# Fewer value orders on TensorE, made later, and promotions wholly on VectorE: a case of a fused attention and MLP kernel

## The chip, the cores and the metric

The kernel runs on one core of a Trainium2 chip. The time is the device time of one execution in microseconds, and all executions compared here are undisturbed ("fast"). A profile shows one execution. Its span leaves out some 1 to 2 us of the device time, so spans are compared with spans and times with times. The "granted clock" is the share of the full TensorE clock that the profile shows as let through: 1.00 is full clock, 0.50 is half clock.

## The reference, cut to what matters

```python
def _attn_ref(q, k, v, f_logit):              # 4 batches, 8 heads, 768 tokens, head size 48
    f = 1.0 / (1.0 + np.exp(-f_logit))
    for t in range(S):
        state = f[:, :, t, :, None] * state + np.einsum('bhd,bhe->bhde', k[:, :, t], v[:, :, t])
        y[:, :, t] = np.einsum('bhd,bhde->bhe', q[:, :, t], state)
# then: tokens x (heads*head size) = 3072 x 384, through an MLP of width 2048
h = x @ w_in
g = h * (1.0 / (1.0 + np.exp(-1.702 * h)))
return g @ w_out
```

The weights arrive as 64 bit numbers, which the kernel itself converts to 32 bits.

## The kernel before

The work is cut into 12 units of 256 tokens. Within a unit the recurrence is done in six levels that double the distance between query and key. In each level TensorE makes scores, VectorE multiplies them with masks ("evacuates" them), and TensorE adds scores times values into the output `y`. A "promotion" multiplies half of the queries and half of the keys by products of the gates, for the next level. Every level needs the rows of v in its own order (`vl`).

Units 0 to 3 are the "fill": the instructions of all engines run in the order of the program, the weights are still being converted (mostly on VectorE), and the MLP of finished units is woven in as "fill" matmuls where its weights are ready. In unit 0 there is no MLP to weave in yet.

The parts that the change touches:

```python
N_FILL = 3
def load_vl(n, u):                       # one order of v for unit n
    if n < N_FILL:                       # by TensorE: permutation matrix times v, copied by ScalarE
        for i, x in enumerate((0, 1) if u == 0 else (u,)):
            pt = ps.tile([P, DM], F32, tag="mm", ...)
            for g in range(NG):
                nc.tensor.matmul(pt[...], lhsT=ident[:, x::2] if u == 0 else perm[:, u - 2, :], rhs=vns[n][:, g, :], ...)
            nc.scalar.copy(vls[n, x], pt)
        return
    ...                                  # from unit 3 on: a DMA from v_tok, a copy of v in DRAM by token
def promote(l):
    if n < N_FILL:
        nc.vector.tensor_tensor(qk[:, 1], qk[:, 1], by[:, 1], ALU.mult)   # key half
        nc.gpsimd.tensor_tensor(qk[:, 0], qk[:, 0], by[:, 0], ALU.mult)   # query half
    else:
        nc.vector.tensor_tensor(qk, qk, by, ALU.mult)
    ...                                  # then ScalarE copies the keys of the next level (Kc)
def level(l):
    ...                                  # scores and sums on TensorE
    promote(l)
    t["A"] = evacuate(256, [(0, l)])     # masks on VectorE
    if n + 1 < N_FILL:
        values(l)                        # the orders of the NEXT unit
def merge(n, fill, columns, share, pieces=0, hold=0, by=1.0):
    ...                                  # deals `columns` of MLP and 5 * `pieces` conversions over the parts of unit n
```

## Time and profile before

| | before |
|---|---|
| time, median of 4 | 727.08 us (725.85 to 729.3) |
| span of the profile | 726.1 us |
| TensorE busy | 695.9 us |
| VectorE busy | 399.6 us |
| GpSimd busy | 62.2 us |
| order matmuls of v (the profile counts each fp32 matmul of the program as two) | 84 |

What bounds the kernel is worked out in the prediction below, with the lines. In a timeline line the columns are: start, length from the first to the last of the group, engine, source line, operation, output<-inputs, shapes, count, and in brackets the idle time ahead and what ended it. In the chain they are start, length and what ran. `tv` are order matmuls, `sc` scores, `y` the output sums, `t` the turning of inputs, `h` and `o` the MLP, `a`, `s`, `w_in` and `w_out` the conversions of weights.

### The profile page before, as it was taken

The page shows a single profiled execution, that of the slowest core. Times are in us where ns is not written, and L with a number is a line of the kernel's source. Part 1 is how long each engine was busy: PE and PEld are TensorE (multiplying, and loading weights), DVE is VectorE, ACT ScalarE, POOL GpSimd, SP SyncE. Part 2 cuts the span into 40 slices and gives each one's busy share as a digit, 9 for nine tenths or more (in the row PEclk, how much of TensorE's full clock was granted, in tenths as well). Part 3 has the DMA queues.
Part 4 walks back from the last instruction along what each step waited for, and adds up shares of the span by engine and source line. Part 5 has one row for each costly group of instructions (what it writes and reads, how often), then busy time and mean ns, then how long its engine had stood idle before and what let it go on. Part 6 is the DMA issues. An engine that isn't in the chain of part 4 may idle for free.

```text
span 726.1 us, 20759 instructions
## 1 busy us (share of the span) xinstructions
PE 695.9 (96%) x9236; PEld 512.4 (71%) x9236; DVE 399.6 (55%) x665; ACT 207.0 (29%) x429; POOL 62.2 (9%) x108
## 2 busy tenths in 40 slices
PE   6876998999999999999999999999999999999998
PEld 5464666677677686686686686686686686686774
DVE  3679966697685754553554554553554554352120
ACT  4443442242222222232232222232232222122120
POOL 4213121210001001001001001001001001000000
PEclk9897999999999999999999999999999999999999
DMA  8565393485126334514513624514413211100000
GB/s 213 137 154 133 78 206 99 119 196 115 47 59 165 117 100 107 136 49 105 140 47 86 152 55 103 146 44 105 133 55 86 67 34 46 34 2 18 29 0 22
DMA packets 65796, 67.88 MB, mean 93 GB/s; under 512 B 29868, under 2 KB 58284, under 8 KB 65708
## 3 DMA queue, kind: packets, MB, share of 16 engines
q1 hardware_dynamic: 65708, 66.57, 36.0%
q8 instruction: 72, 1.18, 0.7%
q14 instruction: 16, 0.13, 0.1%
HBM read 57.11 MB, written 8.26 MB: 90 GB/s over the span
## 4 chain that ended last, share of the span: by engine, by line
PE 90%; DVE 4%; DMA 2%; SPq 2%; issue 1%; ACT 1%; DVEq 0%; ACTq 0%
PE o L614 35%; PE h L598 34%; PE sc L379 7%; PE y L436 6%; PE y L560 2%; PE t L341 2%; DMA bits<-in_moe_w_out_dram 2%; PE sc L520 2%; PE tkn L502 1%; PE tv L277 1%; SPq L243 1%; DMA vn<-in_v_dram 1%; DVE s L208 0%; DVE a L215 0%; DVE w_in L217 0%
## 5 line engine op out<-in xcount | busy, mean ns | idle before, releaser
L614 PE MATMUL o<-w_out,g 128*128 128x384 f32 x768 | 265.8, 495 | 2.7 <-DVE g L604 2.7
L598 PE MATMUL h<-xT,w_in 128*128 128x256 f32 x1152 | 264.4, 383 | 0.0
L598 PEld LDWEIGHTS h<-xT,w_in 128*128 128x128 f32 x1152 | 214.2, 190 | 35.5 <-issue 3.2
L614 PEld LDWEIGHTS o<-w_out,g 128*128 128x128 f32 x768 | 142.2, 191 | 94.5 <-issue 5.6
L604 DVE TENSOR_TENSOR g<-h,sg 128x256 f32<-128x256 f32 x192 | 80.9, 423 | 147.8 <-ACT sg L603 147.1
L603 ACT ACTIVATE sg<-h 128x256 f32<-128x256 f32 x192 | 73.6, 384 | 159.3 <-PE h L598 155.6
L426 ACT COPY Kc<-X 128x512 f32<-128x512 f32 x60 | 37.7, 628 | 166.9 <-DVE X L422 126.3
L422 DVE TENSOR_TENSOR X<-X,tot 128x1024 f32<-128x1024 f32 x45 | 54.9, 1220 | 35.4 <-PE sc L379 35.3
L403 DVE TENSOR_TENSOR A<-sc,masks 128x512 f32<-128x512 f32 (+1 forms) x84 | 62.6, 755 | 8.8 <-PE sc L379 8.8
L436 PE MATMUL y<-A,vl 64*48 64x64 f32 (+1 forms) x2688 | 61.0, 232 | 0.0
L436 PEld LDWEIGHTS y<-A,vl 64*48 64x48 f32 x2688 | 51.3, 122 | 5.8 <-issue 5.7
L368 POOL TENSOR_TENSOR tot<-F 128x512 f32<-128x512 f32 x12 | 12.5, 1041 | 475.3 <-DVE st L541 469.3
L379 PEld LDWEIGHTS sc<-X,Kc 48*64 48x64 f32 x1920 | 34.4, 136 | 23.3 <-issue 21.3
L569 ACT COPY yT<-y 48x512 f32<-48x512 f32 x48 | 27.9, 580 | 73.7 <-PE y L560 73.1
L379 PE MATMUL sc<-X,Kc 48*64 48x64 f32 x1920 | 42.0, 225 | 3.2 <-ACT Kc L426 3.1
L329 DVE STREAM_TRANSPOSE X<-raw 128x1024 f32<-128x1024 f32 x18 | 36.8, 2046 | 7.5 <-PE sc L379 7.1
L379 PEld LDWEIGHTS sc<-X 48*64 48x64 f32 x768 | 19.0, 141 | 23.5 <-issue 15.8
L379 PE MATMUL sc<-X 48*64 48x128 f32 (+1 forms) x768 | 23.7, 261 | 11.4 <-DVE X L373 6.0
L373 DVE TENSOR_TENSOR X<-X,F 128x1024 f32<-128x1024 f32 x12 | 14.8, 1235 | 23.1 <-PE y L560 15.5
L422 DVE TENSOR_TENSOR X<-X,F 128x1024 f32<-128x1024 f32 x9 | 11.0, 1226 | 28.2 <-PE sc L379 28.2
L544 DVE TENSOR_TENSOR st<-st,sc 128x192 f32<-128x192 f32 x44 | 15.6, 354 | 19.6 <-PE sc L520 18.2
L368 POOL TENSOR_TENSOR tot<-tot 128x256 f32<-128x256 f32 (+4 forms) x60 | 24.2, 403 | 4.7
(49 smaller groups left out, 388.1 us busy)
## 6 DMA issues: line engine op xcount, KB each, us to landing
vl<-v_tok SPq DMA_DIRECT2D x45, 192.0 KB, 2.8
bits<-in_moe_w_out_dram SPq DMA_DIRECT2D x8, 768.0 KB, 7.2
bits<-in_moe_w_in_dram SPq DMA_DIRECT2D x8, 576.0 KB, 5.1
xT<-yT SPq DMA_DIRECT2D x24, 144.0 KB, 2.7
raw<-in_f_logit_dram SPq DMA_DIRECT2D x18, 192.0 KB
raw<-in_q_dram SPq DMA_DIRECT2D x18, 192.0 KB, 6.8
raw<-in_k_dram SPq DMA_DIRECT2D x18, 192.0 KB
v_tok<-in_v_dram SPq DMA_DIRECT2D x9, 384.0 KB, 6.9
```

Of the source, the lines that this page charges most:

```text
L329: nc.vector.transpose(out.rearrange("p (a i j) -> p a j i", a=NP, j=R), raw[:, j].rearrange("p a (j d) -> p (a j) d", j=R)[:, :, :32],)
L368: nc.gpsimd.tensor_tensor(tn, t2[:, :, 0], t2[:, :, 1], ALU.mult)
L379: nc.tensor.matmul(out[g * HS:(g + 1) * HS, h, a, :], lhsT=lhs(h, a * U + g * G), rhs=rhs(h, a * U + g * G), start=True, stop=True,)
L403: nc.vector.tensor_tensor(A[:, :, c:c + w].rearrange("p h (x t) -> p h x t", t=64), t["sc"][:, :, c:c + w].rearrange("p h (x t) -> p h x t ...
L422: nc.vector.tensor_tensor(qk, qk, by, ALU.mult)
L426: nc.scalar.copy(Kc.rearrange("p (n m) -> p n m", m=m), X[:, 2].rearrange("p (n two m) -> p n two m", two=2, m=m)[:, :, 0, :],)
L436: nc.tensor.matmul(dst(h, g, a), lhsT=vls[n, u][g * 64:(g + 1) * 64, (2 * a + h) * D:(2 * a + h + 1) * D], rhs=A(h, g, a), start=(start an ...
L569: nc.scalar.copy(yT[rows(h), :, g, :], py[columns(h, g), g])
L598: nc.tensor.matmul(ph, lhsT=w_in[:, c, ff * P:(ff + 1) * P], rhs=xTs[n][:, c, :], start=(c == 0), stop=(c == NK - 1))
L603: nc.scalar.activation(sg, ph, AF.Sigmoid, scale=1.702)
L604: nc.vector.tensor_tensor(g[ff // FG][:, ff % FG, :], ph, sg, ALU.mult)
L614: nc.tensor.matmul(t["po"], lhsT=g[ff // FG][:, ff % FG, tt * P:(tt + 1) * P], rhs=w_out[:, ff, :], start=(ff == ffs[0]), stop=(ff == ffs[ ...
```

## The change

The intent is to take work from TensorE and stop it from standing at a late v: only units 0 and 1 have their orders made by TensorE, and unit 1's are made where unit 1 begins, not inside unit 0. Unit 2's come by DMA. The query halves of the promotions go to VectorE.

```diff
+    N_TURN = 2
 def load_vl(n, u):
-        if n < N_FILL:
+        if n < N_TURN:
 ...                                     (order_v and load_vn likewise)
                 nc.vector.tensor_tensor(qk[:, 1], qk[:, 1], by[:, 1], ALU.mult)
-                nc.gpsimd.tensor_tensor(qk[:, 0], qk[:, 0], by[:, 0], ALU.mult)
+                nc.vector.tensor_tensor(qk[:, 0], qk[:, 0], by[:, 0], ALU.mult)
 ...
-            if n + 1 >= N_FILL:
-                values(l)
+            if n + 1 >= N_TURN:
+                for u in (0, 2) if l == 2 else (l,):
+                    load_vl(n + 1, u)
             promote(l)
             t["A"] = evacuate(256, [(0, l)])
-            if n + 1 < N_FILL:
-                values(l)
 ...
-        if n == 0:
-            parts.insert(2, ("-", lambda: [load_vl(0, u) for u in range(4, NV)]))
-            parts.insert(1, ("-", lambda: [load_vl(0, u) for u in (2, 3)]))
+        if n < N_TURN:
+            parts.insert(2, ("-", lambda: [load_vl(n, u) for u in range(4, NV)]))
+            parts.insert(1, ("-", lambda: [load_vl(n, u) for u in (2, 3)]))
 ...
-            parts.append((kind, lambda: (fn(), begin_q())))
+            parts.append((kind, lambda: (fn(), begin_q(), load_vl(n + 1, 0) if n + 1 < N_TURN else None)))
```

More of the change, by code (lines that the diff above doesn't have):

```diff
@@ L257, in order_v @@
     def order_v(n, engine=nc.sync):
-        if n >= NALL or n < N_FILL:
+        if n >= NALL or n < N_TURN:
             return
@@ L299, in load_vn @@
         vns[n] = (mlp if n == 1 else ld).tile([P, NG, DM], F32, tag="osb" if n == 1 else "vn", name=f"vn_{n}", bufs=1)
-        if n < N_FILL:
+        if n < N_TURN:
             b, s0 = n // NU, n % NU * U
@@ L480, in level @@
                 add(l, slot(t["A"], 0), half(LEV[l - 1], 1))
-            if n + 1 >= N_FILL:
-                values(l)
+            if n + 1 >= N_TURN:
+                for u in (0, 2) if l == 2 else (l,):
+                    load_vl(n + 1, u)
             promote(l)
             t["A"] = evacuate(256, [(0, l)])
-            if n + 1 < N_FILL:
-                values(l)
-        def values(l):
-            for u in (0, 2) if l == 2 else (l,):
-                load_vl(n + 1, u)
         for l in range(2, NL):
@@ L510, in _ @@
             add(NL, slot(t["A"], 0), half(LEV[-1], 1))
-            if n + 1 >= N_FILL:
+            if n + 1 >= N_TURN:
                 load_vl(n + 1, NL)
@@ L525, in _ @@
                             )
-            if n + 2 < N_FILL:
-                load_vn(n + 2)
-            if n + 1 >= N_FILL:
+            if n + 1 >= N_TURN:
                 load_vn(n + 1)
-            else:
-                load_vl(n + 1, NL)
             st = att.tile([P, NC, NP, D], F32, tag="st", name=f"st_{n}", bufs=2)
@@ L666, in parts_of @@
         parts = list(units[n][1])
-        if n == 0:
-            parts.insert(2, ("-", lambda: [load_vl(0, u) for u in range(4, NV)]))
-            parts.insert(1, ("-", lambda: [load_vl(0, u) for u in (2, 3)]))
+        if n < N_TURN:
+            parts.insert(2, ("-", lambda: [load_vl(n, u) for u in range(4, NV)]))
+            parts.insert(1, ("-", lambda: [load_vl(n, u) for u in (2, 3)]))
         if n + 1 < NALL:
```

## The prediction

> **What bounds the kernel now.** I read the page first, then the busy time of each engine in stretches chosen at the borders of the first units, then the chain of waits, then the timelines of VectorE, GpSimd and TensorE between 10 and 160 us. The page's slices (each 18 us) say where there is anything to win:
>
> ```profile
> PE   6876998999999999999999999999999999999998
> DVE  3679966697685754553554554553554554352120
> POOL 4213121210001001001001001001001001000000
> PEclk9897999999999999999999999999999999999999
> ```
>
> After the eighth slice TensorE is full and VectorE is about half full. TensorE is busy 695.9 of 726.1 us, so 30.2 us are idle. The stretches place them: 4.5 at the start, 5.5 in 15 to 28.5, 2.2 in 28.5 to 41, 0.4 in 41 to 53, 7.8 in 53 to 66, 1.0 in 66 to 84, 4.3 in 101 to 117, 1.2 in 135 to 160, 3.3 at the end. From 160 us the end is simply TensorE's remaining work, so whatever the change takes from the first 120 us should reach the end nearly whole.
>
> ```profile
> 15.00:28.50 13.50, 8.03 (x210) 5.04 (x206) 12.36 (x20) 5.69 (x12) 3.50 (x3) 0.87 0.86 206
> 28.50:41.00 12.50, 10.28 (x214) 6.22 (x216) 7.40 (x12) 4.37 (x9) 3.31 (x3) 0.80 0.18 55
> 53.00:66.00 13.00, 5.21 (x128) 4.72 (x127) 12.90 (x21) 4.80 (x9) 6.34 (x8) 0.63 0.66 149
> 66.00:84.00 18.00, 17.04 (x355) 11.21 (x347) 15.92 (x30) 6.47 (x16) 5.04 (x5) 0.98 0.31 89
> ```
>
> The columns after the stretch are busy us (and instructions) of TensorE's matmuls, its weight loads, VectorE, ScalarE and GpSimd, then granted clock, DMA share and GB/s. In unit 0 (4.5 to 53 us) and at the start of unit 1, VectorE sets the pace, except in 28.5 to 41, where it is only 7.4 of 12.5 us busy. The chain shows why:
>
> ```profile
> 9.81 11.14 DMA bits<-in_moe_w_out_dram
> ...
> 24.27 4.21 DMA vn<-in_v_dram
> 28.52 4.39 PE tv L277 x12
> ```
>
> Unit 0 makes the v orders of unit 1 between its levels. That v lands only at 28.5, behind a backlog of other loads, so the TensorE stands at it, and then makes twelve of them at half clock before the next scores at 32.83. VectorE is idle for 6.11 us ahead of the mask multiplication at 33.60.
>
> The second cost is in the split promotions. GpSimd rows first, then VectorE rows of the same times:
>
> ```profile
> 35.73 1.16 POOL L420 TENSOR_TENSOR X<-X,tot 128x512 f32<-128x512 f32 x1 [0.93 <-PE sc L379]
> 39.95 1.15 POOL L420 TENSOR_TENSOR X<-X,tot 128x512 f32<-128x512 f32 x1 [3.06 <-PE sc L379]
> 35.61 1.49 DVE L215 TENSOR_SCALAR a<-s 128x384 int32<-128x384 int32 x2
> 37.49 0.68 DVE L419 TENSOR_TENSOR X<-X,tot 128x512 f32<-128x512 f32 x1
> 40.10 1.21 DVE L212 TENSOR_SCALAR a<-a 128x384 int32<-128x384 int32 x1
> ```
>
> The two L215 take 0.61 together when GpSimd is quiet and one L212 takes 0.34; beside a promotion on GpSimd they take 1.49 and 1.21. The first promotion on VectorE, beside GpSimd's, takes 2.02 instead of 0.68.
>
> **What the skill says.** "SBUF — State Buffer", section "Who interferes with whom", says that VectorE and GpSimd share a port pair, held for a whole instruction while the other fully blocks; an operation with two SBUF inputs contends with a GpSimd operation that reads SBUF. The trace agrees (the rows above; mask multiplications, whose one input is in PSUM, are not stretched: 1.29 us for two at 65.09 beside GpSimd, 1.28 at 20.99). "TensorE: Matmul & The Clock Gate", section "Part 1: The HAM clock gate", says that the array falls to half clock after an idle window of about 3.4 us. The trace agrees roughly, and here a window busy for some 40% is already followed by a slow one: the granted clock is 0.50 to 0.53 in 29 to 32, in 40 to 42 and in 111 to 114. "DMA: Bandwidth & Descriptors", section "Specifications", puts efficient transfers at 512 B and above. The new staging of v moves runs of 48 floats, 192 B; in the trace such a staging landed in 6.9 us median for 384 KB, which I use.
>
> **Part 1, promotions.** VectorE gets 18 halves, each 0.68 us, with the next instruction 0.61 behind: 3.7 us a unit, 11.0 in all. It loses the stretching, which I summed row by row against the unstretched length. Unit 0: 1.34, 1.10, 0.48, 0.46, 0.88, 0.87, together 5.1. Unit 1: 1.33, 0.08, 0.96, 0.91, 0.52, 0.84, together 4.6. Unit 2: 1.30, 0.36, 0.30, 0.44, 0.43, together 2.8. So VectorE's work changes by -1.4, -0.9 and +0.9 us. The halves come ahead of the mask multiplication, so each level's masks come 0.61 later where nothing was stretched, and at level 0 about 0.65 earlier (1.36 instead of 2.02).
>
> **Part 2, v orders in unit 0.** They leave it (28 matmuls, 7 copies). I laid VectorE's order out again from 14.4 us with its own durations. Masks of level 0 end at 16.9 (17.6 now). Those of level 2 end at 24.9, as now, and those of level 3 at 28.4 instead of 34.2, because the wait for v is gone; level 5's at 36.2 instead of 42.4. TensorE then turns unit 1's inputs from about 33.7 instead of 41.9. But between those levels it now does only 1.3 us of scores and sums in each 3.9 us, below the 40%, so I expect it at half clock and charge about 2 us on the turns, which nothing hides. Unit 0's state thus comes some 6 us earlier.
>
> **Part 3, v orders in unit 1.** The first 8 matmuls (1.47 us at full clock, from the row at 11.75) fall in a 4.38 us wait of TensorE, the next 8 in one of 3.42 us; both cost nothing and keep the clock up. I take 1.4 us for that at the scores and sums after 62.94, which ran at 0.50. The last 12 cost about 2.2 us but replace 12 at nearly the same place. The four groups of 4 later in unit 1 (about 0.80 us each, 3.2 together) go. There is a side effect in the program: the fill holds for two parts, and the inserted part counts as one, so it begins one part earlier. That delays level 2's scores by about 2.4 us but takes matmuls from the levels behind. Those levels are then VectorE's (nearly 5.0 us each, now 15.9 busy of 18 in 66 to 84), so about 1 us of the gain is lost there, and is had back where the unit ends under TensorE.
>
> **Part 4, unit 2.** It loses its orders on TensorE altogether: 28 at about 0.19 are 5.3 us of work. It is the same 5.3 us as parts 2 and 3 remove net and is not added again. Its orders become DMA in unit 1: one staging and seven reads, some 2.1 MB more. In 66 to 84 the DMA share is 0.31, so there is room. They are needed only in unit 2, tens of us later. At its start, the conversion stretched to 2.31 at 106.74 loses 1.30 and the promotion adds 0.61: 0.6 earlier.
>
> **Sum.** At the end of unit 0 -6; start of unit 1 -0.65 and -1.4, total about -8; through unit 1 about -9.3 (0.8 for the group of orders ahead of its end, the rest from less fill left); unit 2 -0.6: about -10 us, so 717.5 us. TensorE's side agrees: 5.3 us less work, and some 4 to 5 us of idle time or half clock less in the first 117 us.
>
> **Rivals.** (a) VectorE becomes the bound: promotions are serialised, and every level of units 0 and 1 is lengthened by 0.61. For it: VectorE is at 12.9 of 13 us in 53 to 66. Against it: the stretching was worth more than what is added. It would leave about -4: 723. (b) Orders by DMA get in the way: the in-order queue waits for sums of unit 1 before it can issue weights, or the 192 B runs hold the weights up. For it: queue waits on VectorE for weights are already up to 13 us, and the share is 0.81 in 84 to 101. Against it: the weights wait for the same levels in the program anyway. It would make 722 to 728. (c) The clock: fewer matmuls in unit 0 keep the array cold longer than I charged, 2 to 3 us more: 720. (d) The other way, the waits of 1.62 and 2.67 us at 103 and 109 close and the slow window at 111 goes: up to 4 more, 713.
>
> **Range and chances.** (c) and (d) are about equally likely and (a) and (b) less so, which gives 711 to 723.5. Faster by over 2% means under 712.9, which needs all of (d): 0.1. Slower by over 2% would need a new stall of 25 us, 0.01.
>
> **What would show it.** Right: no wait for v near 28 us; mask multiplication of level 3 near 28; L215, L212 and L217 at their short lengths; GpSimd with 18 fewer instructions; 56 order matmuls instead of 84; TensorE's idle time in 53 to 66 well under 7.8; all after 160 us shifted as a block by about 10. Wrong: if VectorE waits for weights or the queue waits for sums in unit 1; if TensorE's busy sum falls by less than 4; if the gain at unit 1's start is not there at 160 us.

## The result

The changed kernel took 716.7 us (median of 4, 715.02 to 716.99) against 727.08, and 716.27 us in a later control. The ratio of the fast runs is 0.9849, 95% interval 0.982 to 0.9878. Such a ratio is the mean time of one kernel's fast runs over that of the other's of the same rounds, so it is not quite the ratio of the quoted medians. The time of the kernel before varies between 725.6 and 730.8 us, so differences of the changed kernel and its variants are read against each other more safely than against it; differences below about 1 us are not told apart.

| | before | after |
|---|---|---|
| span | 726.1 | 714.7 |
| TensorE busy | 695.9 | 689.5 |
| VectorE busy (instructions) | 399.6 (665) | 397.4 (683) |
| GpSimd busy (instructions) | 62.2 (108) | 39.5 (90) |
| order matmuls | 84 | 56 |
| HBM read and written, MB | 65.4 | 67.5 |

The page's slices of the changed kernel (each 17.9 us; the same four rows as in the prediction):

```profile
PE   6789879999999999999999999999999999999998
DVE  3979778886776655554554554554544644352120
POOL 3020010010000001001001001001001001000000
PEclk9879999999999999999999999999999999999999
```

The first six or seven slices hold everything that changed. The lowered clock is still there, in the second and third digits of its row (8 and 7, where before the second and fourth were 8 and 7). The busy times in stretches whose borders are at roughly the same points of the program as those shown of before:

```profile
15.00:25.00 10.00, 7.77 (x272) 5.41 (x268) 10.00 (x21) 5.55 (x12) 0.00 (x0) 1.00 0.81 213
25.00:34.00 9.00, 4.73 (x140) 4.29 (x142) 9.00 (x19) 2.14 (x4) 0.00 (x0) 0.68 0.70 177
46.00:58.00 12.00, 9.81 (x145) 6.14 (x142) 11.90 (x22) 6.10 (x13) 2.83 (x5) 0.60 0.60 140
58.00:76.00 18.00, 16.61 (x347) 11.39 (x347) 16.53 (x37) 6.81 (x15) 0.00 (x0) 1.00 0.55 148
```

VectorE is busy for all of 15 to 34 us and GpSimd for none of it. At the start of unit 1 (46 to 58) TensorE is idle for 2.2 us of 12, where it was idle for 7.8 of 13. TensorE's rows there, two of before and then four of after, show what fills the waits:

```profile
57.54 1.98 PE L379 MATMUL sc<-X 48*64 48x128 f32 x32 [4.38 <-DVE X L373]
62.94 1.14 PE L379 MATMUL sc<-X 48*64 48x64 f32 x30 [3.42 <-DVE A L403]
44.76 2.26 PE L278 MATMUL tv<-vn,ident 128*64 128x384 f32 x8
49.21 1.99 PE L380 MATMUL sc<-X 48*64 48x128 f32 x32 [2.19 <-DVE X L374]
51.12 2.83 PE L278 MATMUL tv<-vn,perm 128*64 128x384 f32 x8
53.90 1.13 PE L380 MATMUL sc<-X 48*64 48x64 f32 x32
```

The chain of waits shows the same from the other side:

```profile
24.82 0.35 DVE a L213
25.17 0.60 DVE X L420
25.77 0.60 DVE X L421
26.37 0.60 DVE A L404
26.97 0.94 DVE s L209 x2
27.91 0.34 DVE a L216 x2
```

Before, these microseconds were a DMA (v of unit 1) and then order matmuls. Now they are conversions (L213, L209, L216), the two halves of a promotion (L420, L421) and masks (L404), one after the other, at their short lengths. Unit 0 is bound by VectorE.

How far ahead the changed kernel is at the same instruction (start before, start after, difference in us), from the timelines of TensorE and VectorE:

| instruction | before | after | ahead |
|---|---|---|---|
| scores of level 2, unit 0 | 23.44 | 20.99 | 2.45 |
| turning of unit 1's inputs (64 matmuls) | 41.91 | 32.78 | 9.13 |
| first state of unit 0 | 50.47 | 42.14 | 8.33 |
| first scores of unit 1 | 57.54 | 49.21 | 8.33 |
| scores of level 2, unit 1 | 66.56 | 61.33 | 5.23 |
| turning of unit 2's inputs | 86.13 | 75.28 | 10.85 |
| last sums of unit 1 | 99.98 | 89.22 | 10.76 |
| `o` matmuls after the wait in unit 2 | 111.45 | 99.64 | 11.81 |
| last sums of unit 2 | 159.94 | 148.41 | 11.53 |
| end of the span | 726.1 | 714.7 | 11.4 |

Nothing is won or lost after unit 2. Eight of the eleven microseconds come in unit 0 (0.3 of them were there at its first scores, 12.83 against 13.15, ahead of anything that changed). The dip at unit 1's level 2 is the earlier fill (2.42 us) and the last twelve orders (2.16 us), both of which now stand ahead of level 2's scores and stood behind them before. The lead is back at the turning of unit 2's inputs.

### The profile page after: what moved, and what is told of

It reads as the page before. It is cut to its first block, busy times and chain, and to the rows that moved or that the text cites. A ratio compares the mean times of both kernels' runs of the same rounds, so it can differ in the third digit from the quotient of the medians.

```text
span 714.7 us, 20687 instructions
## 1 busy us (share of the span) xinstructions
PE 689.5 (96%) x9208; PEld 509.6 (71%) x9208; DVE 397.4 (56%) x683; ACT 204.4 (29%) x422; POOL 39.5 (6%) x90
## 4 chain that ended last, share of the span: by engine, by line
PE 92%; DVE 7%; issue 1%; DMA 0%; SPq 0%; ACT 0%; DVEq 0%
PE o L606 36%; PE h L590 34%; PE sc L380 7%; PE y L437 6%; PE t L342 3%; PE sc L516 2%; PE tkn L498 1%; PE y L552 1%; PE tv L278 1%; DVE s L209 1%; DVE A L404 1%; DVE X L420 1%; DVE X L421 1%; DVE a L213 1%; DVE a L217 0%
## 5 line engine op out<-in xcount | busy, mean ns | idle before, releaser
L404 DVE TENSOR_TENSOR A<-sc,masks 128x512 f32<-128x512 f32 (+1 forms) x84 | 62.5, 755 | 0.0
L342 PE MATMUL t<-ident,raw 128*64 128x128 f32 x288 | 19.5, 301 | 4.6 <-DMA raw<-in_f_logit_dram 4.6
```

The source lines that it names most:

```text
L342: nc.tensor.matmul(pt[h * HS:(h + 1) * HS, jj, :], lhsT=by_pair[j][:, h, x:x + HS], rhs=ident, start=True, stop=True)
L404: nc.vector.tensor_tensor(A[:, :, c:c + w].rearrange("p h (x t) -> p h x t", t=64), t["sc"][:, :, c:c + w].rearrange("p h (x t) -> p h x t ...
```

## The experiments

All twelve gave correct results. The ratios are to the kernel before in the same rounds. The calls ran on three chips (e5 to e7 on one, e12 on another, the rest on a third), so variants of different calls are compared with this in mind. The runs are, in order, e1 to e12.

**Promotions alone.**

```diff
 (kernel before)
-                nc.gpsimd.tensor_tensor(qk[:, 0], qk[:, 0], by[:, 0], ALU.mult)
+                nc.vector.tensor_tensor(qk[:, 0], qk[:, 0], by[:, 0], ALU.mult)
```

> The kernel before with only the query halves moved to VectorE. Theory (orders do most): unit 0 still stands at the late v near 28 us, so only the stretched rows go: about 2 us gained, 725. Rival (the promotions do most, because VectorE sets the pace in units 0 and 1 and was stretched by 12.6 us in all): 6 us or more gained, 721 or less. Under both, no conversion row of units 0 to 2 is longer than its unstretched length except beside the products of the gates.

726.09 us against 728.28, ratio 0.9981 (0.9958 to 1.0004): about 1.4 us by the ratio, 2.2 by the medians, and the interval includes 1, that is, no change. The rival falls. Unit 0 is no shorter: the turning starts at 42.11. VectorE's timeline of this run says why:

```profile
24.56 0.69 DVE L420 TENSOR_TENSOR X<-X,tot 128x512 f32<-128x512 f32 x1 [1.57 <-PE sc L379]
27.24 0.69 DVE L419 TENSOR_TENSOR X<-X,tot 128x512 f32<-128x512 f32 x1
34.05 0.69 DVE L420 TENSOR_TENSOR X<-X,tot 128x512 f32<-128x512 f32 x1 [6.12 <-PE sc L379]
34.66 0.68 DVE L403 TENSOR_TENSOR A<-sc,masks 128x512 f32<-128x512 f32 x1
```

The 6.12 us of idle time ahead of level 3 stand as before (6.11), because TensorE still waits for v there. What VectorE saved ahead of it became idle time of its own: the 1.57 us for which it stands at the scores of level 2, where before it had no wait.

**Orders alone.**

```diff
 (changed kernel)
-                nc.vector.tensor_tensor(qk[:, 0], qk[:, 0], by[:, 0], ALU.mult)
+                nc.gpsimd.tensor_tensor(qk[:, 0], qk[:, 0], by[:, 0], ALU.mult)
```

> The changed kernel with the query halves back on GpSimd. Theory: 8 us gained of the 10.4, about 719; the stretched conversions are back. Rival (promotions do most): 4 us gained or less, 723 or more. If the two parts' gains add up to clearly less or more than 10.4, they depend on one another.

720.42 us, ratio 0.9902 (0.988 to 0.9925), about 7.1 us by the ratio. The theory holds. By the ratios the parts alone make 1.4 + 7.1 = 8.5 us, and together 11 (0.9849 and, in the control, 0.9844 of 728). So some 2.5 us seem to appear only when both are there. The intervals (about 1.7 us to each side for a part, 2.1 for both) don't by themselves exclude a plain sum. Two other things speak for it: the promotions gain 1.4 to 2.2 us alone, but 3.7 to 4.2 on top of the orders (720.42 against 716.7 and 716.27, with no overlap of the runs); and the place is seen in the trace. VectorE first, then GpSimd, of the run with the orders alone:

```profile
24.78 1.48 DVE L218 TENSOR_TENSOR w_in<-a,s 128x384 f32<-128x384 f32 x2
26.19 1.51 DVE L213 TENSOR_SCALAR a<-a 128x384 int32<-128x384 int32 x2
30.77 1.55 DVE L420 TENSOR_TENSOR X<-X,tot 128x512 f32<-128x512 f32 x1
34.52 1.54 DVE L420 TENSOR_TENSOR X<-X,tot 128x512 f32<-128x512 f32 x1
...
26.31 1.18 POOL L421 TENSOR_TENSOR X<-X,tot 128x512 f32<-128x512 f32 x1 [0.93 <-PE sc L380]
30.40 1.37 POOL L421 TENSOR_TENSOR X<-X,tot 128x512 f32<-128x512 f32 x1 [2.92 <-PE sc L380]
34.43 1.08 POOL L421 TENSOR_TENSOR X<-X,tot 128x512 f32<-128x512 f32 x1 [2.65 <-PE sc L380]
```

The same rows take 1.01, 0.62, 0.68 and 0.68 in the changed kernel. Now that no wait absorbs it, the stretch lengthens unit 0: the turning starts 2.3 us later than in the changed kernel (35.05), and the first state is at 45.27, 3.1 us later. The other 0.9 us are the turning itself, which ran longer at the lower clock (5.72 us against 4.85).

**Orders of three units on TensorE, each where its unit begins.** Unit 2's orders are not replaced by DMA. This tells apart where the orders stand and how many there are.

```diff
 (changed kernel)
-    N_TURN = 2
+    N_TURN = 3
+            if n + 2 < N_TURN:
+                load_vn(n + 2)
```

> The changed kernel, but unit 2's orders too are made by TensorE where unit 2 begins, and no orders come by DMA until unit 3. It separates where the orders stand from how many there are. Theory: 28 matmuls of about 0.19 us come back, the first 8 to 16 of them into TensorE's waits at the start of unit 2: 2.5 to 5 us slower than the changed kernel, 719 to 722. Rival (the DMA orders in unit 1 cost the queue and the weights something): as fast as the changed kernel or faster, 717 or less.

719.64 us, ratio 0.9889 (0.9866 to 0.9912): 2.9 to 3.4 us slower than the changed kernel. The theory holds, and the rival that DMA orders disturb the queue falls. Of the 28 matmuls that came back (TensorE's busy sum is 4.4 us larger, 693.9), the first eight shortened a wait of 1.70 us to 0.55. All 84 are made here and still about seven tenths of the gain of the whole change are there, 8.1 us by the ratio. But this run also has the promotions on VectorE, worth 1.4 to 4.2 us. The place alone is thus worth some 4 to 7 us (an estimate, 8.1 less that), against 2.9 to 3.4 for the number. No run moved the place alone, so that it counts for more than the number is likely and not measured apart.

**The hold of unit 1's fill as before.**

```diff
 (changed kernel)
-    merge(1, fill, UNIT // 2 - LAG // 2, steady, 10, hold=2)
+    merge(1, fill, UNIT // 2 - LAG // 2, steady, 10, hold=3)
```

> The changed kernel with the hold of unit 1's fill counted so that it starts at level 2 again (3 parts instead of 2, since one was inserted). Prediction's step: the earlier fill delays level 2's scores by 2.4 us and is had back by the end of the unit: so here level 2's scores are about 2.4 us earlier and the end is within 1 us of the changed kernel's, 716 to 717.5. Rival (the early fill costs about 1 us for good): 715.5 or less. Third: the early fill fills idle time: 718 or more.

715.36 us (714.53 to 717.49), ratio 0.984: 0.9 to 1.3 us faster than the changed kernel, with overlapping runs. Level 2's scores of unit 1 start 1.8 us earlier (59.57), and the last sums of the unit 1.4 us earlier (87.86). A further 0.5 us lay in the wait in unit 2 and the half clock behind it: there the lead is 1.9 us at the second scores (102.20). The time is in the range of the rival (a lasting cost of about 1 us), and in this profile most of the 1.8 us is not had back by the end of the unit, against the prediction's step. But the runs overlap, and with unit 0 dealt out evenly as well (below) the same edit gained nothing. Whether the earlier fill costs anything for good stays open.

**Useless work on GpSimd beside VectorE.**

```diff
 (changed kernel, after the masks; the line that makes the scratch tile is left out)
+            if n < N_FILL:
+                for h in range(2):
+                    nc.gpsimd.tensor_tensor(shade, A[:, h, :256], A[:, h, :256], ALU.mult)
```

> The changed kernel with useless work on GpSimd: after each level's masks in units 0 to 2 two multiplications of 128x256 that read that level's masked scores and write a scratch that nothing reads. Nothing waits for them. Theory (the two engines block one another at the shared port pair): the conversions right after the masks are stretched by about 0.5 to 0.9 us a level, VectorE's busy sum grows by 8 to 14 us, the end is 4 to 8 us later, 721 to 725. Rival (the stretch came from both halves of one tensor being written at once): VectorE's busy sum within 2 us and the time within 1 us of the changed kernel's.

719.34 us (719.0 to 719.54), ratio 0.9878. VectorE's busy sum is 407.6, 10.2 us more, though it has the same 683 instructions:

```profile
25.03 1.43 DVE L219 TENSOR_TENSOR w_in<-a,s 128x384 f32<-128x384 f32 x2
26.38 1.03 DVE L214 TENSOR_SCALAR a<-a 128x384 int32<-128x384 int32 x2
...
25.25 1.68 POOL L412 TENSOR_TENSOR shade<-A 128x256 f32<-128x256 f32 x2 [3.10 <-DVE A L405]
```

The added operations write a tensor of their own, and no other instruction reads it, yet the conversions beside them are longer: the rival falls. The time rose by only 2.6 to 3.1 us, less than expected. Unit 0's last sums start 3.4 us later (45.92 against 42.55), unit 1's 3.6 us later (92.78 against 89.22): the stretch in unit 1 costs next to nothing. That this is because TensorE has MLP to do there is argued, not tested. The stretch is paid in unit 0.

**Unit 0's conversions dealt out evenly.**

```diff
 (changed kernel)
+    def even(kind):
+        return 3 if kind in "WTB" else 0
-    merge(0, fill, 0, steady, 8)
+    merge(0, fill, 0, even, 8)
```

> The changed kernel with unit 0's 40 weight conversions dealt out evenly over all its parts instead of three to one for the levels: about one less in each level, more in the turns behind them, where VectorE is idle for about 4 us. Theory (VectorE sets unit 0's pace once the wait for v is gone): each level 0.5 us shorter, unit 0 ends about 3 us earlier, 714. Rival (TensorE's turns or loads set it by now): within 1 us of the changed kernel's, 716 to 717.

713.07 us (712.34 to 715.05), ratio 0.9795 (0.9772 to 0.9817). The gain is 3.2 to 3.6 us over the changed kernel. That is the theory's number, but not its place, since unit 0 was to end about 3 us earlier. VectorE's masks of level 5 do end 1.8 us earlier (32.42 against 34.20), but the turning starts only 1.1 us earlier and takes 5.17 us instead of 4.85. The profile is ahead by 0.8 us at unit 0's last sums (41.75), of which 0.3 were there before the edit acts (first scores at 12.49 against 12.83); by 1.3 at unit 1's first scores (47.90), by 2.4 at the turning in unit 1 (72.86) and by 4.1 at the second scores of unit 2 (100.00 against 104.11). The last 1.7 come from eight `o` matmuls that ran at full clock, 2.85 us instead of 4.54. The slow clock was not gone: it fell on the six `o` matmuls ahead of them (3.37 us instead of 2.10), where the wait took it up (0.28 us instead of 1.97). The dealing did not aim at that, so about half of the gain is explained by VectorE's pace and the rest is where the slow clock fell.

**Orders by TensorE for unit 0 only.**

```diff
 (changed kernel)
-    N_TURN = 2
+    N_TURN = 1
-    load_vn(1)
+    if N_TURN > 1:
+        load_vn(1)
```

> The changed kernel with orders by TensorE for unit 0 only; unit 1's come by DMA during unit 0. Theory: TensorE has 5.3 us less work, of which 16 of 28 matmuls stood in waits, so 2 to 3 us gained if the loads land in time, 714. Rival: unit 0's loads are already backed up (DMA share 0.7 to 0.96 up to 34 us), the staging and seven reads push weights and inputs of units 1 and 2 back: 717 to 722.

718.3 us (715.48 to 721.0), ratio 0.986: no gain, with the widest spread of all variants, so the theory of 2 to 3 us falls. TensorE has less work, 688.1 us, but its waits at the start of unit 1 are open again, 4.38 us for the queries and 2.70 for the masks (4.38 and 3.42 before the change). So unit 1's orders stand on TensorE nearly free, and taking them away buys little. Whether the extra loads also delay something, as the rival has it, stays open: this profile was already 1.3 us late at the first scores of unit 0 (14.17), ahead of the new loads, and shows a gap of 2.05 us in the last sums of unit 1 that it puts down to nothing.

**Both edits, even dealing and hold.**

```diff
 (changed kernel, with the even dealing of unit 0)
-    merge(1, fill, UNIT // 2 - LAG // 2, steady, 10, hold=2)
+    merge(1, fill, UNIT // 2 - LAG // 2, steady, 10, hold=3)
```

> Both edits that were faster on their own: unit 0's conversions dealt out evenly, and unit 1's fill held until level 2 again. If the gains (3.6 and 1.3 us by the medians) are of different waits they add: 712 or a little under. If the second was chance of the clock's phase, 713 as with the first alone.

713.68 us (712.46 to 715.47), ratio 0.9816: the same as with even dealing alone (713.07, 0.9795). The hold adds nothing.

**Unit 1's conversions dealt out evenly too.**

```diff
 (the former; merge gets a second share for conversions alone; the lines that sum it are left out)
-            n_ops = min(int(pieces * NOP * at / (by * total)), pieces * NOP) - ops
+            n_ops = min(int(pieces * NOP * dealt / (by * total_dealt)), pieces * NOP) - ops
-    merge(1, fill, UNIT // 2 - LAG // 2, steady, 10, hold=3)
+    merge(1, fill, UNIT // 2 - LAG // 2, steady, 10, hold=3, deal=even)
```

> The former, with unit 1's 50 conversions dealt out evenly too, its fill as before. In the changed kernel VectorE is idle for 3.85 us behind unit 1's turns and TensorE waits 1.4 us for it in the levels. Theory (VectorE sets the pace of unit 1's levels): 1 to 2 us less than the former. Rival (TensorE's fill sets it): the same within 0.7 us.

711.35 us (710.95 to 711.57), ratio 0.9777 (0.9751 to 0.9804): 2.3 us less than the former, a little more than the theory gives. In 55 to 73 us TensorE is now full:

```profile
55.00:73.00 18.00, 18.00 (x388) 13.06 (x382) 17.16 (x37) 7.52 (x16) 0.00 (x0) 0.99 0.51 141
```

That VectorE's pace is the cause is likely, but not shown. In the former's profile VectorE is busy for 17.74 of these 18 us, which speaks for it; but TensorE has no wait there that is put down to VectorE, and its 1.57 us of idle time are put down to nothing ("issue", 0.66 and 0.91 us in the sums). By the end of unit 1 the lead over it is 0.9 us (85.50 against 86.42), and another 0.7 comes at the start of unit 2, where the wait for the queries is 1.95 us instead of 2.42 and two `h` matmuls run at full clock (0.70 us instead of 0.99).

**Useless matmuls to keep the clock up.**

```diff
 (changed kernel, in level(l), ahead of promote)
+            if n == 0 and l + 1 < NL:
+                pt = ps.tile([P, DM], F32, tag="mm", name=f"warm_{l}", bufs=4)
+                for g in range(2 * NG):
+                    nc.tensor.matmul(pt, lhsT=ident, rhs=vns[0][:, g % NG, :], start=True, stop=True)
```

> The changed kernel with four useless matmuls (into a PSUM tile that nothing reads) in each of levels 2 to 4 of unit 0, to keep TensorE busy between the scores. It measures what the half clock costs at the turns, which the prediction put at 2 us. If the array stays at full clock, the 64 turn matmuls take 3.7 us as in unit 1 instead of 4.85, and unit 1 starts about 1 us earlier: 715.5 to 716. If the useless work delays the scores more than that, 717 or more.

717.92 us, ratio 0.9873, 1.6 us slower than the control. The array stayed at full clock:

```profile
32.42 2.85 PE L488 MATMUL warm<-vn,ident 128*128 128x384 f32 x8
35.19 0.69 PE L380 MATMUL sc<-X,Kc 48*64 48x64 f32 x32
35.71 0.63 PE L437 MATMUL y<-A,vl 64*48 64x64 f32 x32
36.27 3.71 PE L342 MATMUL t<-ident,raw 128*64 128x128 f32 x64
```

The turning took 3.71 us, so the half clock costs the changed kernel 4.85 - 3.71 = 1.1 us there. The scores and sums just ahead took 1.08 us (35.19 to 36.27), against 1.92 in the changed kernel (30.86 to 32.78): another 0.8. But eight of the useless matmuls took 2.85 us and delayed the scores of each level, so the cure cost more than the loss: the turning starts at 36.27, and at 32.86 in the control.

**Control: the changed kernel again.** No edit.

> The changed kernel unaltered, as a control in the same call: 716.7, between 715 and 717.

716.27 us (715.06 to 716.61), ratio 0.9844 (0.982 to 0.9868).

**Unit 2's conversions dealt out evenly too.**

```diff
 (the fastest so far)
-    merge(2, fill, UNIT, steady, 8)
+    merge(2, fill, UNIT, steady, 8, deal=even)
```

> The fastest so far (unit 0's and unit 1's conversions dealt evenly, the fill held until level 2), with unit 2's 40 conversions dealt evenly too. TensorE waits for VectorE at the start of unit 2 (1.95 and 1.71 us), where fewer conversions would stand. Theory (VectorE sets the pace there): 1 to 3 us less, 708.5 to 710.5. Rival (from there on TensorE is full, and the waits come back behind the turns, where VectorE has its transposes): within 0.7 us of 711.4.

710.89 us (710.28 to 712.51), ratio 0.9767 (0.9746 to 0.9789), against 711.35: no difference beyond noise. The waits at the start of unit 2 are still 1.95 and 1.70 us, so the theory falls for this unit, and the time is where its rival put it. This version and the former are the fastest, 5 to 6 us faster than the changed kernel. This one is the only kernel whose whole interval lies beyond 2% against the kernel before.

## Why the prediction was right, point by point

**What bounds it.** Right: VectorE sets unit 0's pace once the wait for v is gone. The two single-part runs show it from both sides: with the wait VectorE's saving did not shorten unit 0, and without the wait the 1.9 us by which GpSimd's promotions lengthen VectorE's rows there (5.5 of stretching less six halves of 0.61) came back as a turning 2.3 us later.

**Part 1, promotions.** The sum over all units was right in size: VectorE's busy time fell by 2.2 us, where the working gives 1.4. It held that GpSimd's work beside VectorE was the cause, at a shared port; the useless work on GpSimd shows the first, and the port itself is not seen in any trace. Alone they are worth little. What the prediction did not say is that their worth seems to depend on the other part.

**Part 2, unit 0.** Right in mechanism, and undersized: unit 0's state came 8.3 us earlier, not 6. Two terms were mis-sized. The first is VectorE's order as laid out again. The masks of level 3 ended at 26.97 (predicted 28.4) and those of level 5 at 34.2 (predicted 36.2). From the one to the other the rows of the kernel before, without the stretching and with the halves added, sum to 7.2 us, which is what was measured, where the prediction has 7.8. Nor do its own terms put level 2's masks at 24.9 "as now": with 1.34 and 1.10 us of stretching off and three halves of 0.61 on, they come 0.6 earlier, and 23.7 was measured. The turning thus started at 32.78 (predicted 33.7). The second is the half clock at the turns, which did come: 2 us were charged. Against full clock 1.1 us were lost there, and another 0.8 on the scores and sums just ahead of them. But the turning of the kernel before began at half clock too (45.89 - 41.91 = 4.0 us to the next matmuls, against 4.8), so against it only 0.8 us were lost at the turns.

**Part 3, unit 1.** The two groups of eight did fall into the waits, as predicted, and taking them out again by DMA opened those waits again. But they did not "keep the clock up": the granted clock is 0.60 in 46 to 58, the groups took 2.26 and 2.83 us instead of 1.47, and the stretch from the scores to the fill shortened from 3.8 us (62.94 to 66.7) to 3.0 (53.90 to 56.9), 0.8 us instead of 1.4. Two waits in the levels came up, 0.39 and 1.00 us, where about 1 us was worked out. The charge for the earlier fill was right in kind (1.8 us at level 2's scores by the run with the hold as before, where 2.4 were predicted); whether it leaves a lasting cost is open. The lead at the end of unit 1 was 10.8 us, not 9.3, which is nearly the surplus of unit 0 less the missing clock.

**Part 4, unit 2.** DMA orders were hidden, as predicted: they cost 2.1 MB of traffic, and in unit 2 TensorE waits for none of them. One of the prediction's own signs of being wrong did appear: in unit 1 (46 to 93 us) the DMA queue stands 7.9 us at sums of TensorE before it can issue orders, and the run with three units' orders on TensorE has no such wait. It did no harm that shows, since that run is the slower one and VectorE waits for no weights up to 130 us. Three orders' units on TensorE instead of two cost 2.9 to 3.4 us, which is what this part is worth by itself.

**Unit 2's start.** The conversion went from 2.31 for two to 1.01, and another 1 us was gained up to the `o` matmuls (10.76 to 11.81), where the prediction had 0.6 (1.30 less 0.61, which is rather 0.7). The half clock after the wait stayed: eight `o` matmuls took 4.54 us, so rival (d) did not come. Nor did (a), since the promotions on VectorE gained 3.7 to 4.2 us on top of the orders, nor (b), as said, nor (c), since the half clock in unit 0 cost no more than was charged.

**The sum.** About -10 predicted, -10.4 by the medians and -11.4 by the spans. The errors partly cancelled: unit 0 gave 2 us more, the clock in unit 1 some 0.6 less. That the total came so near is to that extent luck; the places of the gain, unit 0 and the start of unit 1, were foreseen.

## What to carry to other kernels

A wait hides savings of the engines beside it: two edits, one that removes the wait and one that shortens the work in its shadow, can be worth more together than apart, so measure each alone and both. Work that is needed on a full engine is cheapest where that engine waits anyway: here moving it there was worth an estimated 4 to 7 us, and removing a third of it 2.9 to 3.4. When one engine has become the bound of a stage, look next at side work that it carries there and could carry later.

## What the Trainium skill lacked or had wrong

- "TensorE: Matmul & The Clock Gate", "Part 1: The HAM clock gate", names an idle window of about 3.4 us as the cause of the half clock, and says of shorter idles only, without a length, that frequent ones make the clock go up and down. In these runs a partly busy stretch was enough: in the kernel before, TensorE was busy for 1.28 of the 3.4 us up to 39.3, and the granted clock from 40 to 42 was 0.50. That is the 40% of the prediction (its stretch at 29 to 32 followed a wait of 3.48 us with no work, and shows nothing about it), but it is no threshold. In the changed kernel the clock fell after 2.25 busy of the 3.4 us up to 45.4. It fell again after 1.43 of those up to 100.0, but in the run with useless GpSimd work it stayed at 1.00 after 1.42 of those up to 104.4. The two rows, of the changed kernel and of that run, have the same wait ahead:

```profile
99.64 4.54 PE L606 MATMUL o<-w_out,g 128*128 128x384 f32 x8 [1.97 <-DVE g L596]
104.06 2.85 PE L610 MATMUL o<-w_out,g 128*128 128x384 f32 x8 [1.98 <-DVE g L600]
```

- "SBUF — State Buffer", "Who interferes with whom", was borne out in direction. Its clause on two SBUF inputs, on which the prediction leans, does not cover the stretched L212 and L215, which read one tensor; the section's words on `tensor_scalar` do. It gives no lengths for such a pair: beside a GpSimd multiplication of 128x512, 1.06 to 1.86 us long, a VectorE row was longer by up to 1.34 us, and the 18 promotions on GpSimd lengthened VectorE's rows by 12.6 us in the kernel before (the prediction's sum of the rows).
- "DMA: Bandwidth & Descriptors" has no landing time for a copy within DRAM in short runs: 384 KB in runs of 192 B landed in 6.1 us (median of the changed kernel) to 6.9 us (before).
